# Adding the input by accumulating transfers instead of in the eviction, in a ConvNeXt-V2 block

## The chip, the cores and the metric

The kernel runs on one core of a Trainium2 chip. Its engines are TensorE (PE in the profile, with its weight loads as PEld), VectorE (DVE), ScalarE (ACT), GpSimd (POOL) and SyncE (SP, which only issues transfers here). Sixteen DMA engines move data between the chip's memory (DRAM) and the on-chip SBUF; matmul results land in PSUM. SP's transfers go through one hardware queue (q1 in the profile), GpSimd's through a software queue (q0). The metric is the device time of one execution in microseconds; lower is better.

## The reference

The input `x` is an image of 512 x 512 pixels with C = 96 channels in bf16. E = 4C = 384.

```
def reference(x, dw, w1, w2, grn_gamma, grn_beta):
    out = sum over i, j of xp[:, i:i+H, j:j+W, :] * dw[i, j]      # depthwise 3x3, zero padding 1
    h = _layernorm(out, axis=-1)                                   # over the channels, eps 1e-5
    h = gelu(einsum('bhwc,ce->bhwe', h, w1))
    gx = jnp.sqrt((h * h).sum(axis=(1, 2), keepdims=True) + 1e-6)  # per channel, over all pixels
    nx = gx / (gx.mean(axis=-1, keepdims=True) + 1e-6)
    h = grn_gamma * (h * nx) + grn_beta + h
    h = einsum('bhwe,ec->bhwc', h, w2)
    return x + h
```

The sum over all pixels in `gx` forces two phases: nothing of the second einsum can be finished before every `h` is known.

## The kernel before

The image is worked in 128 blocks of 4 rows (`GR = 4`), 2048 pixels each. As a tile with pixels on partitions, a block is 128 partitions x 16 pixels (`PXP`) x 96 channels, which is 3072 contiguous bytes per partition and 384 KB in all.

The first phase, up to about 960 us, does the convolution, the layer norm, the first einsum and the gelu, and collects the sums of squares. It leaves the normalized input of the first einsum in DRAM (`yn_dram`). For 35 blocks it stores the finished gelu in DRAM (`g_dram`, 1536 KB a block), and 5 more stay in SBUF.

Then the scale is folded into the second weight (`W2s`), and the constant that `grn_beta` contributes stands as a row of 96 values, the same on all partitions (`B2bc_f`, copied to `B2c`).

The second phase goes through the 128 blocks in the order `ORDER`. For each one it needs the gelu tile `g`: loaded whole from `g_dram` into `gl` (35 blocks, on GpSimd's queue), held in SBUF (5 blocks), or made again from `yn_dram` (88 blocks: `ynT` loaded in three parts on SP's queue, 12 matmuls of 512 columns on PE, four gelu activations on ACT into `gr`). These loads are issued five blocks ahead (`PRE = 5`) by `load_rest`; for the first five, before the loop. `load_xr` loads the block of the input again as `xr` (384 KB, bf16; GpSimd's queue in the loop), and `stage_xb` on GpSimd adds the constant row to it two blocks ahead, giving `xb` (f32).

`stage_mm2` then does the second einsum: 48 matmuls in four parts of four pixel groups, each part in one PSUM bank, and DVE evicts each part while adding `xb`, into a quarter of the output tile `o_sb` (bf16). Between the parts `pace` puts the matmuls that remake later blocks. `stage_out` stores the tile of the block before on SP's queue, after `stage_mm2` of this block. The last block's tile is stored in quarters by `out_part`, each right after its eviction.

The loop reads

```
        for n, q in enumerate(ORDER):
            sq, pq = (sp, pool) if n < FIRST else (nc.sync, nc.gpsimd)
            if n + PRE < NBLK:
                load_rest(n + PRE, sq, pq)
                load_xr(n + PRE, pq)
            if 3 <= n + 2 < NBLK:
                stage_xb(ORDER[n + 2], pq, B2c)
            ...
            o_sb = stage_mm2(n, q)
            if held:
                stage_out(*held)
            held = (q, o_sb)
```

For the first eight blocks (`FIRST`) the order on SP and GpSimd is the order in which the program is written (`InOrder`); later a scheduler may place these two engines' instructions. The semaphores come from the tile framework: an instruction waits until the tiles it reads are written and the buffer it writes is free. Buffers in the second phase: 5 of `xr`, 3 of `xb`, 3 of `gr`, 2 of `gl`, 4 of `o_sb`. Instructions that go through the wrapper `InOrder` carry its line, L35, in the profile; others carry their own (L283 is `load_xr`, L294 the `gl` load, L328 `stage_xb`, L128 the `ynT` loads, L356 `stage_out`, L1019 `out_part`).

Of the kernel before, what the change touches and what calls it, by code (L numbers as in the profile page):

```python
# [8 lines left out]
ALU = mybir.AluOpType  # L9
# [3 lines left out]
GR = 4  # L13
# [43 lines left out]
def kernel(  # L57
# [10 lines left out]
    nc = tc.nc  # L68
    f32 = mybir.dt.float32
    i32 = mybir.dt.int32  # L70
    bf16 = x.dtype
    assert bf16 == mybir.dt.bfloat16

    B, H, W, C = x.shape
# [6 lines left out]
    NBLK = H // GR  # L81
# [31 lines left out]
    PXP = GR * W // 128  # L113
# [11 lines left out]
    def read_spread(eng, t, q):  # L125
        rows = yn_dram[q].rearrange("(c i) (r w) -> i c r w", i=NI, r=GR)
        for i in range(NI):
            eng.dma_start(out=t[i:128:4], in_=rows[i])  # L128

    def yn_dst(q, r):  # L130
        return yn_dram[q].rearrange("(c i) (r w) -> r c i w", i=NI, r=GR)[r]
# [17 lines left out]
    B2bc_f = consts.tile([128, C], f32, name="B2bc_f")  # L149
# [9 lines left out]
    grp = {}  # L159
# [6 lines left out]
    B2c = consts.tile([128, C], f32, name="B2c")  # L166
# [3 lines left out]
    ORDER = []  # L170
# [14 lines left out]
    p2 = ExitStack()  # L185
    SL = PXP + 2
    with ExitStack() as p1:
        pe, dve, act, pool, sp = (InOrder(tc, e) for e in (nc.tensor, nc.vector, nc.scalar, nc.gpsimd, nc.sync))
# [18 lines left out]
        def out_bank():  # L207
            out_banks[0] += 1
            return PS[:, 7 - out_banks[0] % 2, :GPS * C].rearrange("p (g c) -> p g c", g=GPS)
# [36 lines left out]
        for b in range(min(2, NBLK)):  # L246
# [3 lines left out]
                       in_=zrow[:, None, :NI * GR * 32].to_broadcast([128, 3, NI * GR * 32]), func=ACTF.Identity)  # L250
# [25 lines left out]
        GPS = max(d for d in range(1, cap + 1) if PXP % d == 0)  # L276
        NSUB = PXP // GPS

        def load_xr(n, pq):
            q = ORDER[n]  # L280
            r0 = q * GR
            xr = late.xr.tile([128, PXP, C], bf16, name="xr")
            pq.dma_start(out=xr[:], in_=x[0, r0:r0 + GR].rearrange("r w c -> (r w) c").rearrange(  # L283
                "(p g) c -> p g c", g=PXP))
            grp.setdefault(q, {})["xr"] = xr

        def load_rest(n, sq, pq):
            q = ORDER[n]
            v = grp.setdefault(q, {})
            if is_held(q):  # L290
                v["g"] = gs[q]
            elif is_whole(q):
                v["g"] = late.gl.tile([128, NQ, NCH, QW], bf16, name="gl")
                pq.dma_start(out=v["g"][:].rearrange("p t j w -> p (t j w)"), in_=g_dram[whole.index(q)])  # L294
            else:
                ynt = yn_ring[SLOTS[nth_made[q] % NYT]]
                if q not in KEPT:
                    read_spread(sq, ynt, q)
                v["ynt"], v["w1"] = ynt, w1p if q in KEPT else w1s
# [21 lines left out]
                    c += sz  # L321
            act.activation(out=g[:, t, :, :].rearrange("p j w -> p (j w)"), in_=Uf, func=ACTF.Gelu_apprx_tanh)

        def stage_xb(q, pq, bias):
            if q is None:
                return
            xb = late.xb.tile([128, PXP, C], f32, name="xb")
            pq.tensor_tensor(out=xb[:], in0=grp[q]["xr"][:],  # L328
                                    in1=bias[:, None, :].to_broadcast([128, PXP, C]), op=ALU.add)
            grp[q]["xb"] = xb  # L330

        def stage_mm2(n, q):
            g, xb = grp[q]["g"], grp[q]["xb"]
            GQ = QW // 128
            o_sb = late.o.tile([128, PXP, C], bf16, name="o_sb")
            for sub in range(NSUB):
                O = out_bank()
                for gl_ in range(GPS):
                    gg = sub * GPS + gl_
                    for j in range(NCH):  # L340
                        t, c = gg // GQ, gg % GQ * 128
                        pe.matmul(O[:, gl_, :], lhsT=g[:, t, j, c:c + 128], rhs=W2s[:, j, :],
                                   start=(j == 0), stop=(j == NCH - 1))
                dve.tensor_tensor(out=o_sb[:, sub * GPS:(sub + 1) * GPS, :], in0=O,
                                   in1=xb[:, sub * GPS:(sub + 1) * GPS, :], op=ALU.add)
                if n == NBLK - 1:
                    out_part(q, o_sb, sub)
                if sub == NSUB - 1 and q in nth_made:
                    used[0] += 1
                pace(n, sub)  # L350
            grp.pop(q)
            return o_sb

        def stage_out(q, o_sb):
            r0 = q * GR
            nc.sync.dma_start(  # L356
                out=out[0, r0:r0 + GR].rearrange("r w c -> (r w) c").rearrange("(p g) c -> p g c", g=PXP),
                in_=o_sb[:])

        PRE = 5  # L360
        LEAD = 6
# [12 lines left out]
        def pace(n, sub):  # L374
            soon = (n, sub + 2) if sub < NSUB - 1 else (n + 1, 1)
            due = sum(1 for v in todo if v < soon or v[0] < n)
            even = LEAD + (n * NSUB + sub + 1) * total / (NSUB * NBLK)
            advance(max(due, even), n + PRE)
# [22 lines left out]
        for i in range(NI):  # L401
            dve.tensor_tensor(out=Wd[:, i], in0=eye32[:, None, :].to_broadcast([128, 9, 32]),
                              in1=Ud[:, i, :, None].to_broadcast([128, 9, 32]), op=ALU.mult)
        n = 0
        for h in range(2):
            for j in range(GR):
                for q in (2 * h, 2 * h + 1):
                    a = q + GR * shift(h, j) - j + 1
                    if 0 <= a < 3:
                        n += 1  # L410
                        o, i_ = Wq[32 * q:32 * q + 32, :, :, j, :], Wd[32 * q:32 * q + 32, :, 3 * a:3 * a + 3, :]
# [394 lines left out]
        for k, (b0, n) in enumerate(BATCHES):  # L806
# [16 lines left out]
            for b in range(b0, b0 + n):  # L823
# [8 lines left out]
                last_slot = m  # L832
# [5 lines left out]
        for s in range(last_slot + 1):  # L838
# [112 lines left out]
                combine(b)  # L951
            if s == last_slot - 3:
                pc.close()
                late.xr = p2.enter_context(tc.tile_pool(name="xr", side="right", bufs=5))
                late.xb = p2.enter_context(tc.tile_pool(name="xb", side="right", bufs=3))
                late.gr = p2.enter_context(tc.tile_pool(name="gr", side="right", bufs=GRB))
                late.gl = p2.enter_context(tc.tile_pool(name="gld", side="right", bufs=2))
                late.o = p2.enter_context(tc.tile_pool(name="o", side="right", bufs=4))
            if s == last_slot - 2:
                for n in range(PRE):  # L960
                    load_xr(n, sp)
            if s == last_slot - 1:
                for n in range(3):
                    stage_xb(ORDER[n], pool, B2bc_f)
            if s == last_slot:
                for n in range(PRE):
                    load_rest(n, sp, sp)
# [19 lines left out]
        r = gi[:].bitcast(f32)  # L987
        for it in range(3):
# [5 lines left out]
            r = rn_[:]  # L994
# [19 lines left out]

        advance(LEAD, PRE)
    with p2:
        def out_part(q, o_sb, sub):
            r0 = q * GR
            nc.sync.dma_start(  # L1019
                out=out[0, r0:r0 + GR].rearrange("r w c -> (r w) c").rearrange(  # L1020
                    "(p g) c -> p g c", g=PXP)[:, sub * GPS:(sub + 1) * GPS],
                in_=o_sb[:, sub * GPS:(sub + 1) * GPS])

        held = None
        FIRST = 8
        for n, q in enumerate(ORDER):
            sq, pq = (sp, pool) if n < FIRST else (nc.sync, nc.gpsimd)
            if n + PRE < NBLK:
                load_rest(n + PRE, sq, pq)
                load_xr(n + PRE, pq)  # L1030
            if 3 <= n + 2 < NBLK:
                stage_xb(ORDER[n + 2], pq, B2c)
            if n == NBLK - 1:
                stage_out(*held)
                held = None
            o_sb = stage_mm2(n, q)
            if held:
                stage_out(*held)
            held = (q, o_sb)


# [28 lines left out]
```

## Time and profile before

| | us |
|---|---|
| median of 3 runs | 1464.58 (1464.29 to 1469.97) |
| the profiled execution's own time | 1466.53 |
| its span (first to last instruction) | 1464.7 |

| engine | busy us | share of the span |
|---|---|---|
| PE | 1392.0 | 95% |
| DVE | 1176.8 | 80% |
| ACT | 1404.4 | 96% |
| POOL | 1300.3 | 89% |

The page gives busy time of each engine over the whole span. The two phases use the engines differently, so shares have to be read by stretches. The granted TensorE clock is 0.998 of full speed. The share of DMA is the mean busy share of the sixteen DMA engines. The chain of waits is followed back from the last instruction: at each step to what released it, or to the instruction before it on its engine.

### The profile page before, as it was taken

How to read it: one execution, taken by the hardware profiler on the slowest of the kernel's cores; microseconds unless marked ns; L12 is line 12 of the kernel's file. 1: busy time of each engine (PE TensorE's matmuls, PEld its weight loads, DVE VectorE, ACT ScalarE, POOL GpSimd, SP SyncE). 2: the span in 40 equal slices, each digit the busy share in tenths (PEclk: the TensorE clock that was granted, in tenths of full speed). 3: DMA queues.
4: the chain of work that ended last, by engine and by line, in shares of the span. 5: the costliest groups of instructions: out<-in, count | busy, mean ns of one | idle time of the engine just before them, and what ended most of it. 6: DMA issues, size and time to landing. Idle time of an engine off the chain costs nothing.

```text
span 1464.7 us, 54551 instructions
## 1 busy us (share of the span) xinstructions
PE 1392.0 (95%) x23155; PEld 812.2 (55%) x23155; DVE 1176.8 (80%) x2163; ACT 1404.4 (96%) x1595; POOL 1300.3 (89%) x923
## 2 busy tenths in 40 slices
PE   8889999999999999999999998799999999999998
PEld 3434444444444444444444445567777777777766
DVE  7859989999999999999999998755555555555555
ACT  6889999999999999999999999999999999999997
POOL 2569889999999999999899998469999999999997
PEclk9999999999999999999999999999999999999999
DMA  5577878888888888888878777569999999999997
GB/s 173 166 232 246 252 247 254 259 263 269 256 268 284 248 260 265 273 259 265 257 249 272 247 240 217 171 215 386 348 332 393 393 398 390 402 384 406 388 380 306
DMA packets 167770, 421.66 MB, mean 288 GB/s; under 512 B 34278, under 2 KB 84134, under 8 KB 163046
## 3 DMA queue, kind: packets, MB, share of 16 engines
q1 hardware_dynamic: 151284, 314.59, 65.3%
q0 software_dynamic: 14880, 103.43, 18.6%
q8 instruction: 182, 2.98, 0.8%
q14 instruction: 62, 0.51, 0.1%
q10 hardware_dynamic: 1362, 0.15, 0.1%
HBM read 261.77 MB, written 156.22 MB: 285 GB/s over the span
## 4 chain that ended last, share of the span: by engine, by line
DVE 37%; PE 27%; ACT 13%; POOL 12%; DMA 5%; issue 4%; SPq 1%; ACTq 0%; POOLq 0%; DVEq 0%
PE PS L35 27%; DVE bst L35 26%; POOL xb L328 10%; ACT g L35 8%; DVE xT L35 7%; ACT y_bf L35 2%; DMA out_dram<-o_sb 2%; ACT xT L35 1%; ACT gr L35 1%; SPq L35 1%; POOL xr L283 1%; DMA yn_dram<-yn 1%; DVE y_bf L35 1%; DMA xin<-in_x_dram 1%; DVE o_sb L35 1%
## 5 line engine op out<-in xcount | busy, mean ns | idle before, releaser
L35 ACT ACTIVATE g<-PS 128x512 bf16<-128x512 f32 (+2 forms) x1054 | 718.8, 839 | 13.3 <-PE PS L35 10.1
L35 DVE BATCH_NORM_STATS2 bst<-g 128x6 f32<-128x512 bf16 x1098 | 665.8, 671 | 24.8 <-ACT g L35 24.6
L35 ACT ACTIVATE gr<-PS 128x1536 bf16<-128x1536 f32 x364 | 503.3, 1461 | 15.6 <-PE PS L35 11.0
L35 DVE TENSOR_TENSOR o_sb<-PS,xb 128x384 bf16<-128x384 f32 x512 | 277.7, 556 | 223.2 <-PE PS L35 177.3
L35 POOL TENSOR_TENSOR yn<-y_bf,rbc 128x1536 bf16<-128x1536 bf16 x126 | 391.4, 3109 | 47.2 <-ACT rbc L35 22.8
L328 POOL TENSOR_TENSOR xb<-xr,B2c 128x1536 f32<-128x1536 bf16 x118 | 368.2, 3134 | 1.5
L35 PE MATMUL PS<-xT,Wq 64*32 64x511 bf16 (+1 forms) x9198 | 345.2, 387 | 22.9 <-ACT y_bf L35 6.9
L35 PE MATMUL PS<-ynT,w1p 128*128 128x512 bf16 x1167 | 332.8, 381 | 22.4 <-ACT g L35 4.8
L35 POOL TENSOR_TENSOR ysq<-y_bf 128x1536 bf16<-128x1536 bf16 x114 | 313.4, 2749 | 30.7 <-ACT y_bf L35 17.4
L35 PE MATMUL PS<-ynT,w1s 128*128 128x512 bf16 x1008 | 272.3, 379 | 0.0
L35 PEld LDWEIGHTS <-gr 128*128 128x128 bf16 x4332 | 214.3, 98 | 62.6 <-issue 5.5
L35 PE MATMUL PS<-W2s,gr 128*128 128x96 bf16 x4224 | 223.4, 206 | 4.4 <-DVE o_sb L35 4.3
L35 PEld LDWEIGHTS <-Wq 64*32 64x32 bf16 x9216 | 111.7, 90 | 192.8 <-issue 151.1
L35 ACT ACTIVATE y_bf<-PS 128x1536 bf16<-128x1536 f32 (+2 forms) x135 | 182.2, 1355 | 16.1 <-PE PS L35 14.0
L35 DVE STREAM_TRANSPOSE xT<-xin 128x576 f32<-128x576 f32 (+1 forms) x256 | 181.3, 747 | 13.9 <-DMA xin<-in_x_dram 13.9
L35 PEld LDWEIGHTS <-w1p 128*128 128x128 bf16 x1167 | 89.9, 97 | 177.1 <-issue 105.8
L35 PEld LDWEIGHTS <-g 128*128 128x128 bf16 (+1 forms) x1659 | 102.4, 98 | 87.1 <-issue 56.1
L35 PE MATMUL PS<-w1p,ynT 128*128 128x384 bf16 (+2 forms) x834 | 127.2, 273 | 9.2 <-ACT xT L35 4.2
L35 PE MATMUL PS<-g 128*128 128x128 bf16 x1416 | 119.4, 221 | 3.6 <-DVE PS L35 3.6
L35 PEld LDWEIGHTS <-w1s 128*128 128x128 bf16 x1008 | 81.0, 98 | 40.0
L35 PEld LDWEIGHTS <-gl 128*128 128x128 bf16 x1680 | 83.0, 98 | 28.5 <-issue 7.1
L35 PE MATMUL PS<-W2s,gl 128*128 128x96 bf16 x1680 | 90.2, 206 | 3.9 <-DVE o_sb L35 3.4
(109 smaller groups left out, 723.2 us busy)
## 6 DMA issues: line engine op xcount, KB each, us to landing
xin<-in_x_dram SPq DMA_DIRECT2D x126, 432.0 KB
g_dram<-g SPq DMA_DIRECT2D x105, 512.0 KB
gl<-g_dram POOLq DMA_DIRECT2D x35, 1536.0 KB, 10.9
yn_dram<-yn SPq DMA_DIRECT2D x512, 96.0 KB
ynT<-yn_dram SPq DMA_DIRECT2D x128, 384.0 KB
out_dram<-o_sb SPq DMA_DIRECT2D x127, 384.0 KB
xr<-in_x_dram POOLq DMA_DIRECT2D x123, 384.0 KB, 6.6
ynT<-yn_dram SPq DMA_DIRECT2D x252, 128.0 KB
```

The lines of the kernel that those rows point to most:

```text
L35: r = f(*a, **k)
L283: pq.dma_start(out=xr[:], in_=x[0, r0:r0 + GR].rearrange("r w c -> (r w) c").rearrange("(p g) c -> p g c", g=PXP))
L328: pq.tensor_tensor(out=xb[:], in0=grp[q]["xr"][:], in1=bias[:, None, :].to_broadcast([128, PXP, C]), op=ALU.add)
```

## The change

The input is no longer loaded into a tile of its own, and GpSimd no longer adds the constant row to it. DVE's eviction adds the constant row `B2c` itself (broadcast over the pixel groups). After the next block's `stage_mm2`, GpSimd issues a transfer that reads the block of `x` from DRAM and adds it onto `o_sb` in SBUF (`accum_op=ALU.add`). SP stores the tile three blocks after its add was issued. There are 8 buffers of `o_sb` instead of 4, and none of `xr` and `xb`. The last block's tile is not stored in quarters any more: after the loop it is added, and the tiles that remain are stored. Both transfers see a tile as 128 rows of 1536 contiguous elements (`px_rows`).

```diff
@@ -126,6 +126,9 @@
         rows = yn_dram[q].rearrange("(c i) (r w) -> i c r w", i=NI, r=GR)
         for i in range(NI):
             eng.dma_start(out=t[i:128:4], in_=rows[i])
+
+    def px_rows(ap, r0):
+        return ap[0, r0:r0 + GR].rearrange("r w c -> (r w) c").rearrange("(p g) c -> p (g c)", g=PXP)
 
     def yn_dst(q, r):
         return yn_dram[q].rearrange("(c i) (r w) -> r c i w", i=NI, r=GR)[r]
@@ -276,14 +279,6 @@
         GPS = max(d for d in range(1, cap + 1) if PXP % d == 0)
         NSUB = PXP // GPS
 
-        def load_xr(n, pq):
-            q = ORDER[n]
-            r0 = q * GR
-            xr = late.xr.tile([128, PXP, C], bf16, name="xr")
-            pq.dma_start(out=xr[:], in_=x[0, r0:r0 + GR].rearrange("r w c -> (r w) c").rearrange(
-                "(p g) c -> p g c", g=PXP))
-            grp.setdefault(q, {})["xr"] = xr
-
         def load_rest(n, sq, pq):
             q = ORDER[n]
             v = grp.setdefault(q, {})
@@ -321,16 +316,8 @@
                     c += sz
             act.activation(out=g[:, t, :, :].rearrange("p j w -> p (j w)"), in_=Uf, func=ACTF.Gelu_apprx_tanh)
 
-        def stage_xb(q, pq, bias):
-            if q is None:
-                return
-            xb = late.xb.tile([128, PXP, C], f32, name="xb")
-            pq.tensor_tensor(out=xb[:], in0=grp[q]["xr"][:],
-                                    in1=bias[:, None, :].to_broadcast([128, PXP, C]), op=ALU.add)
-            grp[q]["xb"] = xb
-
         def stage_mm2(n, q):
-            g, xb = grp[q]["g"], grp[q]["xb"]
+            g = grp[q]["g"]
             GQ = QW // 128
             o_sb = late.o.tile([128, PXP, C], bf16, name="o_sb")
             for sub in range(NSUB):
@@ -342,20 +329,18 @@
                         pe.matmul(O[:, gl_, :], lhsT=g[:, t, j, c:c + 128], rhs=W2s[:, j, :],
                                    start=(j == 0), stop=(j == NCH - 1))
                 dve.tensor_tensor(out=o_sb[:, sub * GPS:(sub + 1) * GPS, :], in0=O,
-                                   in1=xb[:, sub * GPS:(sub + 1) * GPS, :], op=ALU.add)
-                if n == NBLK - 1:
-                    out_part(q, o_sb, sub)
+                                   in1=B2c[:, None, :].to_broadcast([128, GPS, C]), op=ALU.add)
                 if sub == NSUB - 1 and q in nth_made:
                     used[0] += 1
                 pace(n, sub)
             grp.pop(q)
             return o_sb
 
-        def stage_out(q, o_sb):
-            r0 = q * GR
-            nc.sync.dma_start(
-                out=out[0, r0:r0 + GR].rearrange("r w c -> (r w) c").rearrange("(p g) c -> p g c", g=PXP),
-                in_=o_sb[:])
+        def stage_add(q, o_sb, eng):
+            eng.dma_start(out=o_sb[:].rearrange("p g c -> p (g c)"), in_=px_rows(x, q * GR), accum_op=ALU.add)
+
+        def stage_out(q, o_sb, eng):
+            eng.dma_start(out=px_rows(out, q * GR), in_=o_sb[:].rearrange("p g c -> p (g c)"))
 
         PRE = 5
         LEAD = 6
@@ -951,17 +936,9 @@
                 combine(b)
             if s == last_slot - 3:
                 pc.close()
-                late.xr = p2.enter_context(tc.tile_pool(name="xr", side="right", bufs=5))
-                late.xb = p2.enter_context(tc.tile_pool(name="xb", side="right", bufs=3))
                 late.gr = p2.enter_context(tc.tile_pool(name="gr", side="right", bufs=GRB))
                 late.gl = p2.enter_context(tc.tile_pool(name="gld", side="right", bufs=2))
-                late.o = p2.enter_context(tc.tile_pool(name="o", side="right", bufs=4))
-            if s == last_slot - 2:
-                for n in range(PRE):
-                    load_xr(n, sp)
-            if s == last_slot - 1:
-                for n in range(3):
-                    stage_xb(ORDER[n], pool, B2bc_f)
+                late.o = p2.enter_context(tc.tile_pool(name="o", side="right", bufs=8))
             if s == last_slot:
                 for n in range(PRE):
                     load_rest(n, sp, sp)
@@ -1014,29 +991,22 @@
 
         advance(LEAD, PRE)
     with p2:
-        def out_part(q, o_sb, sub):
-            r0 = q * GR
-            nc.sync.dma_start(
-                out=out[0, r0:r0 + GR].rearrange("r w c -> (r w) c").rearrange(
-                    "(p g) c -> p g c", g=PXP)[:, sub * GPS:(sub + 1) * GPS],
-                in_=o_sb[:, sub * GPS:(sub + 1) * GPS])
-
-        held = None
+        held, added = None, []
         FIRST = 8
         for n, q in enumerate(ORDER):
             sq, pq = (sp, pool) if n < FIRST else (nc.sync, nc.gpsimd)
             if n + PRE < NBLK:
                 load_rest(n + PRE, sq, pq)
-                load_xr(n + PRE, pq)
-            if 3 <= n + 2 < NBLK:
-                stage_xb(ORDER[n + 2], pq, B2c)
-            if n == NBLK - 1:
-                stage_out(*held)
-                held = None
             o_sb = stage_mm2(n, q)
             if held:
-                stage_out(*held)
+                stage_add(*held, pq)
+                added.append(held)
+            if len(added) > 3:
+                stage_out(*added.pop(0), sq)
             held = (q, o_sb)
+        stage_add(*held, nc.gpsimd)
+        for v in added + [held]:
+            stage_out(*v, nc.sync)
 
 
 # ---- launch: one core; inputs and outputs as the reference has them ----
```

## The prediction

> **What bounds the kernel now.** The change touches the second phase, so I first cut the span into stretches. Columns: busy time and count of PE, PEld, DVE, ACT and POOL, granted clock, DMA share, GB/s.
>
> ```profile
> 950.00:1000.00 50.00, 47.30 (x645) 34.36 (x644) 28.31 (x79) 48.06 (x36) 35.70 (x24) 1.00 0.68 235
> 1000.00:1050.00 50.00, 50.00 (x736) 37.22 (x733) 28.55 (x53) 49.35 (x37) 47.73 (x29) 1.00 0.98 373
> 1050.00:1100.00 50.00, 50.00 (x738) 37.20 (x735) 28.33 (x52) 49.53 (x36) 47.43 (x27) 1.00 0.94 343
> 1100.00:1200.00 100.00, 99.02 (x1444) 73.29 (x1442) 55.76 (x103) 97.74 (x72) 96.73 (x61) 1.00 1.01 393
> 1200.00:1300.00 100.00, 97.87 (x1428) 72.43 (x1427) 54.84 (x102) 96.17 (x71) 96.75 (x58) 1.00 1.01 396
> 1300.00:1400.00 100.00, 97.82 (x1429) 72.37 (x1427) 54.53 (x101) 96.33 (x70) 97.05 (x60) 1.00 1.01 390
> 1400.00:1440.00 40.00, 37.62 (x550) 27.80 (x549) 21.06 (x40) 37.34 (x28) 38.07 (x24) 1.00 1.01 390
> 1440.00:1465.00 25.00, 20.19 (x325) 15.71 (x322) 13.66 (x26) 16.01 (x12) 16.72 (x8) 0.99 0.68 259
> ```
>
> Four things are nearly full at once: PE 98%, ACT 96%, POOL 97%, and the sixteen DMA engines at 1.01 from 1100 us on. Only DVE has room (55%). PE is full until 1100 and then loses 0.98 + 2.13 + 2.18 + 2.38 = 7.7 us up to 1440. Next, who held it up: the chain of waits, restricted to 940 to 1465 us, by line.
>
> ```profile
> by line: PE PS L35 54.4%; POOL xb L328 26.8%; DMA out_dram<-o_sb 6.3%; issue 3.1%; POOL xr L283 3.0%; ACT gr L35 2.9%; DVE o_sb L35 1.8%; POOL gl L294 0.8%; DVE W2s L35 0.1%; DVE sc L35 0.0%; DVEq L35 0.0%; DVE den L35 0.0%; POOLq L294 0.0%
> ```
>
> PE carries it to 1129 us, then GpSimd's bias add, then three stores that held `o_sb` buffers (13.40, 10.03 and 9.87 us long). So GpSimd does bind, but only by those 7.7 us: PE is just behind it. Last, the DMA queues and issues in 1100 to 1430.
>
> ```profile
> DMA packets 30594, 129.44 MB, mean 392 GB/s; under 512 B 5799, under 2 KB 5799, under 8 KB 27218
> ...
> q0 software_dynamic: 10446, 73.82, 57.8%
> q1 hardware_dynamic: 20100, 54.92, 42.4%
> ...
> gl<-g_dram POOLq DMA_DIRECT2D x26, 1536.0 KB, 11.1
> xr<-in_x_dram POOLq DMA_DIRECT2D x84, 384.0 KB, 6.7
> ```
>
> The queues' shares add up to the whole time of the engines, so each byte has a price. GpSimd's queue: 0.578 x 330 us / 73.82 MB = 2.58 us per MB; SP's queue: 0.424 x 330 / 54.92 = 2.55. A 384 KB tile (0.393 MB) thus takes 1.01 us of all sixteen engines, loaded or stored. 84 blocks in 330 us is 3.93 us a block, of which an `xr` load is a quarter.
>
> **The change part by part.**
>
> *Bias adds on GpSimd go.* 118 at 3135 ns and 7 at 3125 ns are 391 us of GpSimd time, all in the second phase. On the path it is worth at most the 7.7 us that PE idles; beyond that PE and ACT hold the end. DVE's 36.4 us of waits for `xb` lie inside that.
>
> *DVE's eviction* stays the same instruction on 128x384 from PSUM (556 ns); its second operand becomes `B2c` broadcast. Taken at nothing: DVE has 45% free to cover it, and 512 evictions could each grow by 0.35 us before DVE reached PE's pace (0.45 x 3.93 us / 4 = 0.44 us less margin).
>
> *The `xr` loads go*: 123 through GpSimd's queue, 5 on SP before 950 us. 123 x 1.016 = 125 us of DMA time leave the second phase. GpSimd's issues (553 ns each) are replaced one for one by those of the adds; if an accumulating issue cost more, GpSimd, now otherwise idle, hides up to 3 us of it per block.
>
> *128 accumulating transfers come.* No row shows one. Such a transfer does all that the load did, since it fetches the same x and writes the same tile, so it can't cost less than 1.01 us; that excludes a gain. It must also fetch the old `o_sb`, and the nearest row for fetching a tile from SBUF is the store, 1.00 us. If an engine handles the two fetches one after the other, as every row says it does with all other bytes (both queues' shares sum to 1.00, not more), an add is 1.016 + 1.00 = 2.02 us. Upper end: the price per MB of the first phase, 83.8% x 690 us / 180.27 MB = 3.21 us (small packets), is 1.25 times the present one; twice a tile at that price is 2.5 us. Lower end: the second fetch hides entirely, 1.01. I take 2.02, the sum of the two rows that it consists of.
>
> The Trainium skill (Collectives: The Full Stack, "The bandwidth ceiling: the fold count and why AG ≠ RS ≠ AR") speaks against the change: a reducing transfer is slower not for the addition but because it issues two source reads on the same ring, measured there at 1.93 times a copy. By it an add would be an estimated 1.96 us and the total below some 8 us lower; no run here shows an accumulate yet.
>
> *New waits.* GpSimd: add n-1 waits for DVE's fourth eviction of block n-1; queued behind it are the `gl` loads of block n+6, wanted five blocks later (landing 11.1 us against 5 x 3.93 = 19.7 us): no cost. SP: the store of block n-4 waits for its add, issued three blocks earlier (11.8 us at today's pace; `xr` lands in 3.4 to 10.0, median 6.6). Behind it on SP are the `ynT` loads, five blocks ahead. As long as landing stays within three blocks, no cost; a longer landing eats the `ynT` lead of two more blocks first. `o_sb` lives about six blocks out of eight buffers; the four waits of DVE for a store (7.6 us) go or move into the DMA total.
>
> *The end.* Now the last eviction ends at 1461.45 us and its quarter store is out by 1464.7. Afterwards the whole last tile is added (0.55 issue + 3.4, the shortest landing) before its store: about 4.5 us more.
>
> *The sum.* DMA time in the second phase today, share by stretch: 34.0 + 49.0 + 47.0 + 303 + 40.4 + 17.0 = 490 us of the 515 from 950 on; 25 are unfilled at both ends. Afterwards 490 - 125 + 128 x 2.03 = 625 us, which at a share of 1.01 takes 619. That exceeds what PE and ACT need (about 500), so DMA sets the pace: 4.9 us a block. Unfilled: the early blocks' adds fill some 9 us of the start, the end adds 4.5, so 25 - 9 + 4.5 = 20. End: 950 + 619 + 20 = 1589, say 1590. The profiled execution took 1466.53 against a span of 1464.7 and a median of 1464.58: span and median agree within 0.2 us, so the span's sum stands for the median.
>
> **The rivals.**
>
> *Accumulating at the price of a load* (second fetch hidden, 1.01 us). For it: nothing in the trace forbids a fetch from HBM and one from SBUF at a time. Against: per-MB prices are equal in both directions and no stretch shows a share over 1.01. Then DMA need is 490 + 5 us, PE gets its 7.7 us back, the end costs 4.5: 1464.6 - 7.7 + 4.5 = 1461. This is the case that is not slower. It decides up to a price of about 1.1 loads: each tenth of a load is 13 us of DMA, and some 10 to 15 us of unfilled time at the start is all that can take it. With ACT's idle time back as well (13 us in 1050 to 1440) it could reach 1456.
>
> *The engine doesn't overlap an add's fetches with its write.* Then three passes, 3 x 1.01 = 3.0 us per add: 1590 + 128 x 1.0 = 1720. For it: the write needs both fetches complete, unlike in a copy. Against: packets of other rows can run meanwhile. It decides from about 2.5 us on.
>
> *SP's store blocks the loads.* Adds share GpSimd's queue with `gl` loads (1536 KB, 4 us of DMA each), so landing could exceed three blocks; then `ynT` is late and PE waits, on top of the DMA total. `xr` lands at most 10.0 us after issue today, DMA-bound perhaps 15, about the 14.7 us of three blocks at 4.9. Price: a `ynT` landing per some blocks, 30 to 60 us: about 1635.
>
> **How the numbers follow.** DMA-bound at about twice a load, 0.68; price of a load, 0.16; three passes, 0.11; SP blocking on top, 0.05. The forecast is the likeliest: 1590. Its own range, for prices of 1.6 to 2.5 loads, is 1538 to 1655 (130 us per load's price). The range 1462 to 1655 takes in most of the price-of-a-load case and leaves out its lower part (0.07) and three passes (0.11). A measurement of this kernel can tell some 0.5% (7.3 us) from no change; in the price-of-a-load case the gain of 3.6 us lies within that, so I give it 0.04 faster, 0.10 same, 0.02 slower. All others are slower: 0.68 + 0.11 + 0.05 + 0.02 = 0.86.
>
> **What would show it.** Right: span near 1590; DMA share 1.0 in every stretch from about 985 us to the end; GpSimd's queue rising from 58% to about 65% of the engines; PE falling to about 80% in 1100 to 1400 with waits on `gl` or `ynT` landing; POOL busy only for issues; the chain of waits led by DMA lines, no `xb`. Wrong: PE still at 98% or more and a share near 1.0 (an add costs a load); or GpSimd's queue over 75% of the engines (three passes); or a DMA share well under 1 with SP waiting for adds (the queue's order, not the bytes).

## The result, and the profile after

The changed kernel takes 1568.63 us (median of 4 runs, 1564.89 to 1569.27) against 1464.43 us before: a ratio of 1.070, 95% interval 1.0666 to 1.0733. It is 104 us slower; 1590 was forecast, with a range of 1462 to 1655. The profiled execution took 1564.89 us, the shortest of the four, with a span of 1563.1. In the experiments below, each ratio is to runs of the kernel before that were made together with that experiment (median 1466.5 us, and 1466.3 for the last three kernels).

The stretches of the second phase, columns as in the prediction's first view (busy time and count of PE, PEld, DVE, ACT and POOL, granted clock, DMA share, GB/s):

```profile
950.00:1000.00 50.00, 47.30 (x644) 34.29 (x643) 28.12 (x79) 48.07 (x36) 8.86 (x11) 1.00 0.66 175
1000.00:1050.00 50.00, 47.04 (x665) 34.80 (x663) 25.38 (x47) 44.93 (x34) 11.46 (x14) 0.97 1.06 316
...
1100.00:1200.00 100.00, 85.31 (x1212) 62.34 (x1209) 46.65 (x86) 82.21 (x60) 21.52 (x28) 0.98 1.05 327
1200.00:1300.00 100.00, 82.44 (x1153) 60.72 (x1152) 44.64 (x83) 79.10 (x57) 21.93 (x28) 0.97 1.05 328
1300.00:1400.00 100.00, 87.75 (x1177) 63.70 (x1176) 45.52 (x84) 79.65 (x58) 21.51 (x28) 0.92 1.05 320
...
1540.00:1564.00 24.00, 8.63 (x163) 7.34 (x160) 6.97 (x14) 4.56 (x4) 3.41 (x4) 0.79 0.81 219
```

GpSimd went from 97% to 21%, but PE and ACT fell with it, to about 85% and 80%. The one column that stays full is the DMA share, from 1000 us to 1540. The GB/s beside it fell (393 to 327 in 1100 to 1200): the engines are busier and move fewer counted bytes. Where the time went is in the DMA queues and issues in 1100 to 1430:

```profile
q0 software_dynamic: 12947, 61.03, 67.3%
q1 hardware_dynamic: 16741, 45.71, 36.9%
...
gl<-g_dram POOLq DMA_DIRECT2D x21, 1536.0 KB, 10.5
o_sb<-in_x_dram POOLq DMA_DIRECT2D x70, 384.0 KB, 12.0
```

GpSimd's queue takes 67.3% of the engines for 61.03 MB, where it took 57.8% for 73.82. And 70 adds were issued in this stretch, where 84 `xr` loads were before: 4.71 us a block instead of 3.93. The add lands after 12.0 us, the `xr` load took 6.7.

The chain of waits from 950 us on, by line, and who waited for whom in 1000 to 1540 us (total, times, longest):

```profile
by line: PE PS L35 30.3%; DMA ynT<-yn_dram 29.8%; DMA out_dram<-o_sb 29.0%; issue 3.7%; DMA o_sb<-in_x_dram 2.5%; POOL o_sb L340 0.8%; ACT gr L35 0.8%; DVE o_sb L35 0.4%; POOLq L1035 0.1%; POOL gl L289 0.1%; DVE W2s L35 0.1%; POOLq L340 0.1
```

```profile
DVE o_sb L35 <- PE PS L35: 278.2, 313, 6.2
POOL o_sb L340 <- DVE o_sb L35: 278.0, 74, 10.1
ACT gr L35 <- PE PS L35: 96.7, 69, 5.3
...
PE PS L35 <- DMA ynT<-yn_dram: 68.5, 32, 4.4
```

GpSimd has left the chain; transfers carry over 60% of it. PE waits for `ynT`, and ACT and DVE wait for PE. The transfers that the chain names are loads and stores, the adds only with 2.5%: my reading is that the adds take the engines' time and the others come late for it, which the experiments test. The chain names who was last, not who used the resource.

### The profile page after: what moved, and what is told of

Same layout as the page of the kernel before. It is cut to its first block, busy times and chain, and to the rows that moved or that the text cites. A ratio compares the mean times of both kernels' runs of the same rounds, so it can differ in the third digit from the quotient of the medians.

```text
span 1563.1 us, 54519 instructions
## 1 busy us (share of the span) xinstructions
PE 1414.3 (90%) x23155; PEld 824.7 (53%) x23155; DVE 1177.2 (75%) x2163; ACT 1407.5 (90%) x1595; POOL 946.6 (61%) x800
## 4 chain that ended last, share of the span: by engine, by line
DVE 36%; DMA 28%; PE 18%; ACT 8%; issue 4%; POOL 3%; SPq 2%; POOLq 0%; ACTq 0%; DVEq 0%
DVE bst L35 26%; PE PS L35 18%; DMA ynT<-yn_dram 12%; DMA out_dram<-o_sb 11%; DVE xT L35 7%; ACT g L35 5%; SPq L35 2%; ACT y_bf L35 1%; POOL yn L35 1%; ACT gr L35 1%; DMA yn_dram<-yn 1%; DMA xin<-in_x_dram 1%; DMA o_sb<-in_x_dram 1%; DVE y_bf L35 1%; ACT xT L35 1%
## 5 line engine op out<-in xcount | busy, mean ns | idle before, releaser
L35 DVE TENSOR_TENSOR o_sb<-PS,B2c 128x384 bf16<-128x384 f32 x512 | 278.2, 558 | 311.6 <-PE PS L35 299.7
L35 PE MATMUL PS<-ynT,w1s 128*128 128x512 bf16 x1008 | 283.3, 391 | 72.2 <-DMA ynT<-yn_dram 68.5
L340 POOL DMA_DIRECT2D o_sb<-in_x_dram x121 | 104.1, 860 | 342.4 <-DVE o_sb L35 295.5
L35 PEld LDWEIGHTS <-gr 128*128 128x128 bf16 x4332 | 224.2, 101 | 62.9 <-issue 9.5
L35 PE MATMUL PS<-W2s,gr 128*128 128x96 bf16 x4224 | 232.7, 211 | 0.5 <-DVE o_sb L35 0.2
```

The lines of the kernel that those rows point to most:

```text
L35: r = f(*a, **k)
L340: eng.dma_start(out=o_sb[:].rearrange("p g c -> p (g c)"), in_=px_rows(x, q * GR), accum_op=ALU.add)
```

## Experiments

**Plain loads instead of adds.**

```diff
-  eng.dma_start(out=o_sb..., in_=px_rows(x, q * GR), accum_op=ALU.add)
+  eng.dma_start(out=o_sb..., in_=px_rows(x, q * GR))
```

> The changed kernel, but the transfer onto o_sb is a plain load of x instead of an accumulating one: same bytes named, same queue, same order and waits; the output is then x alone. Theory (engine time: an accumulating row costs 252 ns where a plain one costs 117, so the DMA engines are the bound): DMA need falls by 128 x 1.02 = 130 us, PE sets the pace again, 1455 to 1466 us, price per tile 1.0 us. Rival (order: SP's stores wait for the transfer issued three blocks before, GpSimd's adds wait for DVE, and the loads queued behind come late): the order is untouched, so it stays near 1568, certainly above 1540.

Measured: 1465.76 us, ratio to the kernel before 0.9998 (0.9980 to 1.0016), at the upper edge of what was expected. The whole slowdown goes with one argument; queue, order and waits are in the program as they were. Its stretches:

```profile
1100.00:1200.00 100.00, 100.00 (x1475) 74.73 (x1474) 56.51 (x105) 99.07 (x73) 18.74 (x35) 1.00 1.01 393
1200.00:1300.00 100.00, 98.62 (x1443) 73.21 (x1441) 55.98 (x104) 97.43 (x71) 18.20 (x34) 1.00 1.01 395
1300.00:1400.00 100.00, 96.37 (x1407) 71.33 (x1404) 54.07 (x100) 95.39 (x70) 17.68 (x33) 1.00 1.01 392
...
1440.00:1467.00 27.00, 16.15 (x266) 12.71 (x262) 11.33 (x21) 12.01 (x9) 3.22 (x6) 0.86 0.82 313
```

PE is back, but not at 100% throughout: at a DMA share of 1.01 it still loses 5 us in 1200 to 1400, 3.9 of them waiting for `ynT`. GpSimd's add is gone here too, and no time is won.

**Two plain loads for each add.** As above, and each block loads the same bytes once more into a tile that nobody reads.

```diff
+  junk = late.x2.tile([128, PXP * C], bf16, name="x2")
+  eng.dma_start(out=junk[:], in_=px_rows(x, q * GR))
```

> As plain_load (output x alone), and each block also loads the same 384 KB of x a second time into a tile that nobody reads, on the same queue. Theory (an add costs as much engine time as two transfers of the tile, and nothing else about it matters): two loads are 2 x 1.01 = 2.02 us per block, so the time is that of the changed kernel, 1550 to 1580. Rival (the accumulation itself, its latency or its wait, sets the time): no accumulation is left and nothing waits for the second load, so it is near plain_load, at most 1500.

Measured: 1565.53 us (2 runs), ratio 1.0675 (1.0644 to 1.0705), against 1568.63 and 1.0700 with adds: the intervals overlap. Two of its stretches, and GpSimd's queue in 1100 to 1430:

```profile
1100.00:1200.00 100.00, 78.41 (x1042) 56.64 (x1041) 40.77 (x75) 71.99 (x52) 30.60 (x58) 0.91 1.02 412
1200.00:1300.00 100.00, 84.40 (x1085) 61.01 (x1084) 41.56 (x77) 73.36 (x53) 28.39 (x53) 0.89 1.02 412
```

```profile
q0 software_dynamic: 14972, 90.89, 67.7%
```

An add costs the time of two transfers of its tile: GpSimd's queue takes 67.7% of the engines here and 67.3% with adds. Here both transfers are counted, at 412 GB/s. In the changed kernel, 107.32 MB in the 330 us from 1100 are 325 GB/s; if each of the 70 adds is counted as a second tile (27.5 MB), they are 408.

One premise of the rival wasn't met: something does wait for the second load, GpSimd itself before it issues the next one (86.5 us in 1000 to 1440). With the DMA engines at 1.02 I take that for a consequence of the full engines, not a cause.

**Stores seven blocks later**, with 12 buffers.

```diff
-  if len(added) > 3:
+  if len(added) > 7:
```

> The changed kernel with the stores seven blocks after the add instead of three, and 12 buffers of o_sb instead of 8. Theory (engine time): the bytes are the same, 1560 to 1575. Rival (SP's stores block the ynT loads behind them: SP waited 37.8 us for adds, and PE 68.5 us for ynT): the adds have long landed when the store comes up, so 30 to 70 us are won, 1500 to 1540.

Measured: 1565.94 us (2 runs), ratio 1.0677 (1.0647 to 1.0708): no gain beyond the spread of the runs. SP's own waits in 1000 to 1540 us, in the changed kernel and then in this one:

```profile
SPq L128 <- DMA out_dram<-o_sb: 141.8, 62, 4.0
SPq L343 <- DMA out_dram<-o_sb: 79.3, 36, 4.5
SPq L128 <- DMA ynT<-yn_dram: 67.7, 110, 2.3
SPq L343 <- DMA o_sb<-in_x_dram: 37.8, 13, 8.1
```

```profile
SPq L128 <- DMA out_dram<-o_sb: 140.7, 55, 4.2
SPq L343 <- DMA out_dram<-o_sb: 87.5, 34, 4.3
...
SPq L343 <- DMA o_sb<-in_x_dram: 14.0, 5, 6.1
```

The stores' wait for adds falls from 37.8 to 14.0 us, and SP waits for other transfers instead (PE's wait for `ynT` is 60.8 us, against 68.5 in the changed kernel). The rival of the store queue falls.

**No transfer of x at all.** `stage_add` does nothing.

> The changed kernel without any transfer of x in the second phase; the output is h without x. Theory (engine time): another 125 us of DMA time go, but PE and ACT set the pace already without accumulation, so within 0.5% of plain_load, 1452 to 1462. Rival (DMA still binds at the price of a load, as its share of 1.01 in the kernel before would suggest): 15 us or more below plain_load, under 1445.

Measured: 1460.25 us, ratio 0.9956 (0.9940 to 0.9972). That is where it was expected, 5.5 us (0.4%) below `plain_load`, about what PE still lost there. One stretch is enough:

```profile
1200.00:1300.00 100.00, 100.00 (x1476) 74.68 (x1475) 56.55 (x105) 99.13 (x73) 4.22 (x8) 1.00 0.83 298
```

With the DMA share at 0.83, PE never waits in this stretch. So the whole way of the input through this phase, adds and transfers together, was worth 0.44% to the kernel before.

**Adds for half and for an eighth of the blocks**, plain loads for the rest.

```diff
+  more = dict(accum_op=ALU.add) if q % 2 else {}        # an eighth: if q % 8 == 1
-  eng.dma_start(..., accum_op=ALU.add)
+  eng.dma_start(..., **more)
```

> The changed kernel with accumulating transfers for the odd blocks only; even blocks get a plain load onto o_sb (their output is x alone). Theory (engine time): half of the extra 128 x 1.02 us, so about halfway between plain_load (1465.8) and the changed kernel (1568.6): 1505 to 1530. Rival (a fixed cost of having any accumulating transfer in the queue): 1545 or more.

> As half_added, with accumulating transfers for every eighth block (16 of 128). Theory (engine time, no room left): plain_load already runs at a share of 1.01 and loses PE time to late ynT loads, so 16 x 1.02 = 16 us come through nearly in full, 1474 to 1484. Rival (10 to 15 us of unfilled DMA time at the start take them, as the prediction's threshold of 1.1 loads has it): 1463 to 1469.

Measured: 1513.25 us with half (ratio 1.0318, 1.0292 to 1.0343) and 1475.31 with an eighth (1.0060, 1.0038 to 1.0081). Above `plain_load` that is 9.6 us for 16 adds, 47.5 for 64 and 102.9 for 128: 0.60, 0.74 and 0.80 us each. The half is where it was expected. With the eighth, the time lies above the whole range of the rival (1463 to 1469), so 16 adds already cost something. But by the two ratios' intervals the 9.6 us can be anything from about 5 to 14, where 16 were put in: some 2 to 11 us of room were there, where the prediction's threshold of 1.1 loads rests on 10 to 15, and whether the price of one add grows with their number isn't shown. The trace of the eighth shows the mechanism already, PE waiting for `ynT` in 1000 to 1440 us (3.9 us in `plain_load`):

```profile
PE PS L35 <- DMA ynT<-yn_dram: 11.7, 9, 2.1
```

**Without GpSimd's add and without accumulation**, everything computed: `xr` loaded as before (7 buffers), DVE adds it in a second instruction per quarter, 8 buffers of `o_sb`.

```diff
+  dve.tensor_tensor(out=o_sb[:, part, :], in0=O, in1=B2c..., op=ALU.add)
+  dve.tensor_tensor(out=o_sb[:, part, :], in0=o_sb[:, part, :], in1=xr[:, part, :], op=ALU.add)
```

> GpSimd's add removed without accumulation, everything computed: xr is loaded as in the kernel before (7 buffers), DVE evicts each quarter with B2c and then adds the quarter of xr to it in bf16; quarter stores at the end as before; 8 buffers of o_sb. Theory (DMA and PE both full): the bytes are those of the kernel before and PE regains at most its 7.7 us; plain_load's last eviction came 4.2 us earlier than the kernel before's, and its longer end is gone, so 1459 to 1463, 0.1 to 0.4% faster. Rival (DVE's longer eviction, some 0.3 us more per quarter, delays the PSUM banks and so PE): 1470 or more.

Measured: 1465.41 us, ratio 0.9992 (0.9978 to 1.0005): neither expectation, no difference. DVE's two instructions and the stretches:

```profile
L35 DVE TENSOR_TENSOR o_sb<-PS,B2c x512: 548/551/559, 963.9 to 1461.4; 128x384 bf16<-128x384 f32 x171
L35 DVE TENSOR_TENSOR o_sb<-o_sb,xr x512: 357/358/360, 964.5 to 1462.0; 128x384 bf16<-128x384 bf16 x171
```

```profile
1100.00:1200.00 100.00, 97.61 (x1427) 72.45 (x1425) 87.43 (x204) 96.43 (x71) 18.03 (x34) 1.00 1.01 389
1200.00:1300.00 100.00, 100.00 (x1470) 74.46 (x1468) 89.72 (x209) 99.08 (x72) 18.20 (x34) 1.00 1.02 408
...
1400.00:1440.00 40.00, 37.52 (x533) 27.95 (x532) 32.25 (x76) 35.66 (x27) 6.43 (x12) 0.96 0.97 374
```

GpSimd's 391 us of adds became 183 us of DVE (512 x 358 ns). PE fills 1200 to 1300, but loses 2.4 us in 1100 to 1200 and 2.5 in 1400 to 1440. The last eviction of a quarter starts at 1461.4 us, against 1460.9 before. What PE waits for has changed, in 1000 to 1440 us, before and then here:

```profile
PE PS L35 <- DVE o_sb L35: 7.3, 16, 2.0
```

```profile
PE PS L35 <- DMA ynT<-yn_dram: 5.4, 4, 2.5
```

Before, PE waited for DVE, which waited for `xb` (36.4 us) and for stores (7.6). Here it waits for `ynT`, and 2.4 and 2.5 us of that fall into just the two stretches where it loses time. So one wait took the other's place. No version that computes everything beat the kernel before.

## Why the prediction was right, point by point

*The mechanism held.* DMA became the bound, because an add costs two transfers: `plain_load` takes the slowdown away, `two_loads` brings it back without any accumulation, and the cost grows with the number of adds. That the engine must fetch the old tile from SBUF as well is the reading that fits these; the trace doesn't show that fetch by itself.

*The price of an add* was forecast at 2.02 us from a load and a store. In the trace's packet records a packet of an add is one row of 3072 bytes and takes 252 ns in the median; before, a packet of the `xr` load held two rows and took 234. So 128 rows x 252 ns / 16 engines = 2.02 us, 2.15 times the 0.94 us of a load at its median. The engines' time in all goes by the means, which the few slow packets raise for the load more than for the add: 256.5 and 258.9 ns, or 2.05 and 1.04 us, a factor of 1.98. The smaller packet alone isn't the reason: the five `xr` loads that SP issued before 950 us have one row to a packet on the other queue, and take 121 ns a row in the median. Behind it stands the Trainium skill (Collectives: The Full Stack, "The bandwidth ceiling: the fold count and why AG ≠ RS ≠ AR"): its direction holds here, and its factor of 1.93, measured there between two collectives, is near the 1.98 of the means.

*The DMA time in all* was forecast at 625 us. From 950 us to the end the share is 1.01 over 614 us, that is 620. `plain_load` has 0.95 x 517 = 491, so the adds brought 129 us, where 130 were forecast.

*The filling was mis-sized*; it is the step that made 1590 out of the 1563 of the profiled execution (1568.6 in the median). The prediction let 625 us pass at a share of 1.01 (619) with 20 us unfilled at the ends, 639 from 950 us on. It took 614. The unfilled ends were right: 17.0 us up to 1000 and 4.6 from 1540. But the share between them was 1.05, which no row of before showed, so 567 us of packet time passed in 540 instead of 561. The other 5 us are the 620 for 625. That is most of why 1.0 us more of engine time per add cost only 0.80. Sixteen engines can only show a share above 1 where packet records overlap, and with adds they overlap more: in 1100 to 1430 us more than sixteen packets are open at once for 48.5% of the time, against 24.7% before, 25.2% in `plain_load` and 27.2% in `two_loads`. Since `two_loads` needs the same time at 1.02, I take the 0.03 between them for part of an add's record that hides beside other packets; what hides is not shown.

*The end* was forecast 4.5 us longer (its terms, 0.55 and 3.4, add up to 3.95) and is 10: the last eviction ends at 1549.8 and the span at 1563.1, 13.3 us later (3.2 before). The last add is issued at 1550.1 and its store starts at 1559.3, so add and waiting took about 9 us. The shortest landing of `xr` was the wrong row for a full queue.

*GpSimd's adds* were to be worth at most 7.7 us. They are worth nothing that can be measured: `dve_adds` and `plain_load` do without them, at 0.9992 and 0.9998. In `plain_load` the last eviction does end 4.2 us earlier (1457.3 for 1461.45), and the longer end takes that back. In `dve_adds` PE waits for `ynT` in place of `xb`, so I read the DMA engines, at 1.01, as the next in line. The 26.8% that `xb` had of the chain before was the share of one of several that were equally late.

*The waits* cost nothing, as forecast: the store's wait for the add (`stores_later`), and GpSimd's wait for DVE, which at 278 us is long and harmless with GpSimd at 21% (`plain_load` has 253.7 us of it in 1000 to 1440 and loses nothing). An issue on GpSimd rose from 553 to 860 ns, hidden as said. DVE's eviction stayed the same (556 to 558 ns).

*The rivals.* The price of a load was forecast at 1461, `plain_load` gave 1465.8: PE got back less than 7.7 us, and from the last eviction at 1457.3 to the end of the span at 1467.0 it takes 9.7 us. (The prediction says that its range takes in most of that rival; but the range begins at 1462, and the rival's own 1461 lies outside it.) Three passes fell with the price of 2.02. Of the signs, GpSimd's queue at 67.3% (65 forecast), PE waiting for `ynT` and no `xb` came true; PE at 85% stands for the 80 forecast. By the number of its matmuls in 100 us it is 81 to 84% of before (1153 to 1212 where 1427 to 1444 were); each took longer, those on `ynT` 391 ns for 379, in stretches where the granted clock was 0.92 to 0.98.

## What to carry to other kernels

An accumulating transfer isn't a free addition: here it took twice the DMA time of the load that it replaced. Before work is moved from an engine to the DMA queues, add up the queues' shares in that stretch; at a sum of 1.0 most of an added microsecond of engine time shows (here 0.74 us of each 1.0 with half the blocks added, 0.80 with all). And where four resources are at 96% or more, taking one out of the chain is worth only its distance to the next.

## What was not expected of the hardware

The DMA share reached 1.04 to 1.06 where every block is added (1.03 with half), against 1.02 at most without adds. The counted bytes of an add are those of one tile, so the GB/s column falls (393 to 327) while the engines are full: a rate read without the share would have looked like room. And the granted clock of PE fell to between 0.92 and 0.98 in the stretches where PE was starved (0.89 in one of `two_loads`), against 1.00 before; the 512-column matmuls on `ynT` took 391 ns instead of 379. Since PE waited for transfers there, I take it for a consequence; no run holds the clock apart.
